# A chunked linear-attention and squared-ReLU kernel: half of W1 in two wider loads, u and w by other engines, and another order of all steps

## The chip, the core and the metric

The kernel runs on one core of a Trainium2 chip. The metric is device time in microseconds (us), as a median over runs; lower is better. Before the change it is 173.49 us (three runs, 173.22 to 173.87).

In the profile PE is TensorE's matmul unit, PEld its weight load, DVE is VectorE, ACT is ScalarE, POOL is GpSimd and SP is SyncE, which here only issues transfers. A "q" behind an engine's name (SPq, POOLq) is its sequencer, which waits and issues.

## What is computed

For 4 batches and 8 heads of 768 time steps with 48 channels, a recurrence with a decayed state, and then a two-layer network with a squared ReLU on its output (3072 rows of 384):

```python
for t in range(S):
    cur = einsum('bhd,bhe->bhde', u * k[t], v[t])
    y[t] = einsum('bhd,bhde->bhe', r[t], state + cur)
    state = w[:, :, None] * state + einsum('bhd,bhe->bhde', k[t], v[t])
x = y as (3072, 384)
h = maximum(x @ w_in, 0)          # w_in: 384 x 2048, called W1 in the kernel
out = h * h @ w_out               # w_out: 2048 x 384, called W2
```

Inputs and output are float32; the matmuls of the kernel take bfloat16.

## The kernel before

**Units.** The 768 steps are cut into 6 chunks of 128, which with 4 batches gives 24 units; unit i is batch i mod 4, chunk i div 4. Each unit goes through the same steps, each named by a method of class `Do`, with its unit behind it (`A.7` is step A of unit 7):

- `ld.r`, `ld.k`, `ld.v` (line 387) load the unit's 128 x 8 x 48 values, 192 KB in runs of 48 floats.
- `kh`, `rh` (424, 430) scale k and r by powers of w into `rk`. Units 0 to 3 read these powers from PSUM, where `WkQ` and `WtQ` write them; later ones from SBUF (`WkS`, `WtS`).
- `T` and `Tc` (454, 466) transpose r and k on TensorE and copy them to SBUF as `rkT`; from unit 7 on `XB` (473) does this by a transposing transfer.
- `A` (476) makes the products of k and r within the chunk, `Bm` (501) masks them, in two halves `.0` and `.1`; `Y` (509) multiplies with v (`vb`, line 451, is v as bfloat16) and adds the part from the state.
- `P0`, `P1`, `du`, `dv` (436 to 446) make the term with u: r times k, times u, summed over channels, times v. `xs` (559) adds it to Y.
- `U` (536) makes the unit's share of the state; `S0`, `ts`, `S` (566 to 572) carry the state on with the decay `WLm`.
- `X` and `xTc` (575, 580), or `xX` (584) by a transposing transfer, give x transposed.

**The network** works on groups of units: `GROUPS` makes group 0 and 1 of one unit each (units 0, 1) and groups 2 to 12 of two (units 2 and 3, 4 and 5, and so on). `F1.g.s` (587) is 12 matmuls of 128 columns for a group of one unit or 6 of 256 for one of two, `re` (599) takes the maximum with 0 and `sq` (606) squares. A group of one unit has 4 F1 steps, one of two has 8. F1.g.s of a group of two needs slice s of W1; of a group of one it needs slices 2s and 2s+1. `F2.i.f.4` (615) adds 4 of unit i's 16 products with W2, from slice f/4 of it; `os` (652) copies the sum and `out` (657) stores it. The last unit is done in two parts (`F2c`).

**The weights.** W1 is 8 slices of 256 columns. `lW.0.s` (393) loads a slice through SP, 384 KB in runs of 1 KB, into a staging buffer `st`, and `cW.0.s` (403) casts it; slice 2 is cast by the transfer itself, which GpSimd issues (`W.0.2`, line 416). W2's four slices come that way, too (`W.1.0` to `W.1.3`). `lQ.q` (400) can load slices 2q and 2q+1 at once; with `WIDE` empty it isn't used.

**w and u.** `w` (314) and `u` (323) load the two tables as rows, and the shuffles `shw`, `shu` (320, 329) spread them over all partitions. `wc` (361) loads w a second time, as a column, in two transfers of single elements, and `WLcol` (370) takes its power by 128.

**Fillers.** `Z.n.b` (643) does matmuls of the identity worth n times 128 columns into bank b, in 512-column matmuls and a rest of 128-column ones. Their result is not read.

**Order.** `ORDER` (line 24) is one list of 951 steps. Each is `name:engine/buffers`: A is ScalarE, D VectorE, G GpSimd, P TensorE, S SyncE's transfer queue; the digits choose buffers or PSUM banks. The loop at line 676 issues them in this order, so each engine runs its own steps in the list's order; semaphores enforce what the data and the buffers ask.

```python
for step in ORDER.split():
    what, how = step.split(":")
    ...
    getattr(Do, name)(E[eng[0]], *at, *map(int, eng[1:]))
```

The first steps of each engine that matter here, in the list before:

```
SP      ld.r.3 ld.k.0 ld.r.0 u ld.r.1 ld.k.3 ld.r.2 ld.k.1 ld.k.2 lW.0.1 ld.v.0 ld.v.3 lW.0.5 ld.v.1 lW.0.0 lW.0.4 ld.v.2 lW.0.6 lW.0.7 lW.0.3 wc ld.r.4 ld.k.4 ld.k.5 ld.r.5 ld.v.5
GpSimd  P0.0 P1.0 P1.3 vb.3 dv.3 dv.0 vb.1 P0.2 P1.2 dv.1 cW.0.4 W.0.2 dv.2 W.1.0 cW.0.3 WLm W.1.1 kh.4 W.1.2
VectorE shw shu rh.0 rh.3 kh.3 kh.0 du.0 P0.3 kh.1 rh.1 kh.2 du.3 P0.1 P1.1 rh.2 du.1 cW.0.1 Bm.0.1 Bm.1.0 Bm.0.0 Bm.3.1 Bm.3.0 xs.0 Bm.1.1 xs.3 xTc.0 du.2 xs.1 Bm.2.0 xTc.1 Bm.2.1 cW.0.6 cW.0.7 xs.2 xTc.2
TensorE Z.66.7 T.3 T.0 Z.22.7 A.0 T.1 A.1 A.3 U.3 T.2 Y.0 U.0 A.2 Y.3 X.0 Y.1 X.3 F1.0.0 X.1 F1.0.2 F1.1.2 F1.1.0 Y.2 U.2 F1.1.3 X.2 F1.0.3 F1.2.0 F1.2.3 F1.2.1 F1.0.1 F1.2.7 F1.2.6 F2.3.0.4
```

## Time and profile before

| what | value |
|---|---|
| median of three runs | 173.49 us (173.22 to 173.87) |
| the profiled execution | 174.07 us |
| its span, first to last instruction | 172.3 us |
| TensorE matmuls | 161.7 us busy, 94% of the span, x1691 |
| VectorE | 139.9 us, 81% |
| ScalarE | 104.5 us, 61% |
| GpSimd | 88.2 us, 51% |
| moved by transfers | 29.13 MB, mean 169 GB/s |

Matmuls overlap in TensorE's pipeline, so its busy time is no measure of a peak. Of an idle time only that of the engine that bounds a stage costs anything, so the profile is read by stages: busy time in stretches of the span, the chain of waits that ended last, and the waits of the engine that is full. The line numbers in the profile are those of the listing above.

### The profile page before, as it was taken

The numbers are of one execution on the slowest core, as the hardware profiler recorded it, in microseconds if no ns is written. First come the engines' busy times: TensorE is split into PE (matmuls) and PEld (weight loads), VectorE is DVE, ScalarE is ACT, GpSimd is POOL, SyncE is SP. The second block draws the span as 40 slices with busy tenths as digits, with TensorE's granted clock in tenths as the row PEclk, the third lists the DMA queues.
The fourth block names the chain that finished last, engine by engine and source line by source line (L and its number), as shares of the span: only waits on it lengthen the run. The fifth ranks groups of instructions, "written<-read, shape, count | busy, mean of one in ns | idle before, by whom it ended". The sixth has DMA issues, their size and how long they took to land.

```text
span 172.3 us, 4337 instructions
## 1 busy us (share of the span) xinstructions
PE 161.7 (94%) x1691; PEld 121.6 (71%) x1691; DVE 139.9 (81%) x272; ACT 104.5 (61%) x187; POOL 88.2 (51%) x105
## 2 busy tenths in 40 slices
PE   3976899999999997999999999999999999999993
PEld 1445788776787776777687696886686786878772
DVE  5599887569999996788999899779989889682731
ACT  3475477694599485467569276595596454553740
POOL 5425967215857497998339402879922872000000
PEclk9995699999999999999999999999999999999999
DMA  5999999999697998999999997999595963130322
GB/s 99 218 230 257 330 211 192 202 147 224 112 204 153 209 205 190 231 194 183 238 176 211 185 206 140 230 159 234 132 130 107 127 136 98 44 93 0 141 91 91
DMA packets 105588, 29.13 MB, mean 169 GB/s; under 512 B 98008, under 2 KB 105568, under 8 KB 105568
## 3 DMA queue, kind: packets, MB, share of 16 engines
q1 hardware_dynamic: 103672, 26.95, 76.2%
q0 software_dynamic: 1744, 1.77, 6.8%
q8 instruction: 13, 0.21, 0.5%
q10 hardware_dynamic: 152, 0.14, 0.2%
q14 instruction: 7, 0.06, 0.1%
HBM read 20.46 MB, written 4.72 MB: 146 GB/s over the span
## 4 chain that ended last, share of the span: by engine, by line
PE 71%; SPq 10%; DMA 7%; ACT 5%; DVE 2%; issue 2%; POOL 1%; POOLq 0%; ACTq 0%
PE bank L622 31%; PE bank L594 29%; SPq L388 5%; SPq L396 4%; DMA st<-in_moe_w_in_dram 4%; DMA ldv<-in_v_dram 3%; PE bank L494 3%; ACT hr L602 2%; PE bank L531 2%; ACT hq L609 2%; PE bank L527 2%; PE bank L552 2%; PE bank L636 2%; PE bank L578 1%; DVE S0W L567 1%
## 5 line engine op out<-in xcount | busy, mean ns | idle before, releaser
L594 PE MATMUL bank<-xT,W 128*128 128x256 bf16 (+1 forms) x624 | 71.2, 266 | 0.4 <-DVE W L288 0.3
L622 PE MATMUL bank<-W,hq 128*128 128x384 bf16 x368 | 68.5, 326 | 0.3 <-DVE S0W L567 0.3
L594 PEld LDWEIGHTS <-W 128*128 128x128 bf16 x624 | 56.1, 99 | 9.0 <-DVE W L288 0.5
L602 ACT ACTIVATE hr<-bank 128x512 bf16<-128x512 f32 x70 | 40.6, 593 | 27.5 <-PE bank L594 26.8
L609 ACT ACTIVATE hq<-hr 128x512 bf16<-128x512 bf16 x72 | 43.6, 626 | 7.3 <-DVE hr L604 6.1
L622 PEld LDWEIGHTS <-hq 128*128 128x128 bf16 x368 | 33.9, 98 | 19.2 <-ACT hr L602 0.5
L507 DVE TENSOR_TENSOR Bm<-bank,maskJT 128x512 bf16<-128x512 f32 x48 | 31.1, 678 | 0.6 <-PE bank L494 0.6
L604 DVE TENSOR_SCALAR hr<-bank 128x512 bf16<-128x512 f32 x26 | 17.6, 686 | 11.7 <-PE bank L594 9.7
L441 POOL TENSOR_TENSOR P<-P,ub 128x384 f32<-128x384 f32 x14 | 15.0, 1072 | 16.2 <-DVE P L437 15.9
L434 POOL TENSOR_TENSOR rk<-ldr,Wt 128x384 bf16<-128x384 f32 x13 | 13.8, 1063 | 7.8 <-DMA ldr<-in_r_dram 7.8
L449 POOL TENSOR_TENSOR dv<-ldv,du 128x384 f32<-128x384 f32 x16 | 13.9, 878 | 2.8 <-DVE du L444 2.8
L560 DVE TENSOR_TENSOR xs<-bank,dv 128x384 bf16<-128x384 f32 x24 | 13.1, 552 | 2.0 <-PE bank L531 0.9
L444 DVE TENSOR_REDUCE du<-P 128x8 f32<-128x384 f32 x24 | 12.9, 545 | 1.6 <-POOL P L441 1.3
L286 ACT COPY os<-bank 128x384 f32<-128x384 f32 x13 | 5.9, 487 | 13.4 <-PE bank L622 13.4
L573 POOL TENSOR_TENSOR S0W<-ts,WLm 128x384 bf16<-128x384 f32 x9 | 9.4, 1053 | 8.7 <-DVE ts L570 8.6
L428 POOL TENSOR_TENSOR rk<-ldk,Wkhat 128x384 bf16<-128x384 f32 x12 | 12.8, 1076 | 2.0 <-DMA ldk<-in_k_dram 1.9
L531 PE MATMUL bank<-vb,Bm 128*128 128x48 bf16 x192 | 11.6, 187 | 1.5 <-DVE Bm L507 0.9
L613 DVE TENSOR_TENSOR hq<-hr 128x512 bf16<-128x512 bf16 x24 | 12.4, 523 | 0.3
L288 POOL CAST vb<-ldv 128x384 bf16<-128x384 f32 x10 | 6.1, 606 | 12.7 <-DMA ldv<-in_v_dram 11.5
L437 POOL TENSOR_TENSOR P<-ldr,ldk 128x384 f32<-128x384 f32 x10 | 10.6, 1066 | 3.4 <-DMA ldr<-in_r_dram 3.4
L531 PEld LDWEIGHTS <-Bm 128*128 128x128 bf16 x192 | 9.9, 99 | 2.6 <-DVE Bm L507 1.7
L288 DVE COPY os<-bank 128x384 f32<-128x384 f32 (+2 forms) x12 | 6.2, 518 | 6.0 <-PE bank L622 2.7
(67 smaller groups left out, 163.7 us busy)
## 6 DMA issues: line engine op xcount, KB each, us to landing
ldr<-in_r_dram SPq DMA_DIRECT2D x24, 192.0 KB, 4.0
ldk<-in_k_dram SPq DMA_DIRECT2D x24, 192.0 KB, 3.7
ldv<-in_v_dram SPq DMA_DIRECT2D x24, 192.0 KB, 4.2
out_dram<-os SPq DMA_DIRECT2D x23, 192.0 KB, 2.3
st<-in_moe_w_in_dram SPq DMA_DIRECT2D x7, 384.0 KB, 5.6
W<-in_moe_w_out_dram POOLq DMA_DIRECT2D x4, 384.0 KB, 7.2
rkT<-rk SPq DMA_TRANSPOSE x17, 3.7
W<-in_moe_w_in_dram POOLq DMA_DIRECT2D x1, 192.0 KB, 5.1
```

The costliest lines, as they stand in the source:

```text
L434: e.tensor_mul(scaled("r", i), loaded("r", i), early("WtQ") if i < EARLY else Wt2)
L441: e.tensor_mul(t, t, ub)
L444: e.tensor_reduce(dub[slot[f"dv{i}"]], P0b[slot[f"P{i}"]], axis=mybir.AxisListType.X, op=ALU.add)
L449: e.tensor_mul(dvb[slot[f"dv{i}"]], loaded("v", i), t)
L507: e.tensor_mul(o, a, mask_b)
L531: e.matmul(y[:, hc, D * h : D * (h + 1)], m[h][:, hc, :], vb[:, 2 * hc + h, :], start=(i < B), stop=True, skip_group_check=True,)
L560: e.tensor_add(xsb[slot[f"xs{i}"]].rearrange("p (a b) -> p a b", a=HP), heads(bank(f"bY{i}"), 2 * D), dvb[slot[f"dv{i}"]].rearrange("p (a ...
L594: e.matmul(hp[:, fi, :], W1[f // 2][:, c, 128 * (f % 2) : 128 * (f % 2 + 1)], xt[:, c, :], start=(c == 0), stop=(c == CCH - 1), skip_group ...
L602: e.activation(hr, hp, AF.Relu)
L604: e.tensor_scalar_max(hr, hp, 0.0)
L609: e.activation(hq, hr, AF.Square)
L622: e.matmul(bank(f"bO{i}")[:, 0:d_model], hqb[slot[f"hq{g},{f // m}"]][:, at : at + L], W2[f // 4][:, f % 4, :], start=(summed[i] == 1), st ...
```

## The change

The same steps compute the same values. What differs:

- `WIDE = (2, 3)`: slices 4 to 7 of W1 come by `lQ.2` and `lQ.3`, two loads of 768 KB in runs of 2 KB, into two buffers `sw`, instead of four `lW`. The four casts read from there.
- `u` is issued by GpSimd instead of SP.
- `WCP = True`: `wc` is eight products on TensorE of a row of `logw` with a single 1, into a PSUM bank; `WLcol` then needs only one step for each half. The two transfers of single elements are gone.
- `st` has 5 buffers instead of 6, `hq` 29 instead of 30.
- `ORDER` is another list of 956 steps: other places, other engines and other buffers for nearly all. By engine: `re` 62 on ScalarE and 34 on VectorE (70 and 26 before); `P0` 14 on GpSimd and 10 on VectorE (10 and 14); `P1` 16 and 8 (14 and 10); `dv` 19 and 5 (16 and 8); `cW` 3 ScalarE, 1 VectorE, 3 GpSimd (2, 3, 2); `os` 16 ScalarE and 9 VectorE (13 and 12). Nine fillers worth 131 x 128 columns replace two worth 88.
- Other edits rewrite options that neither version uses (paired units, `DUO`, loads of two units at once), and the mask tile's name.

The first steps of each engine in the new list:

```
SP      ld.r.0 ld.k.0 ld.k.3 ld.r.3 ld.r.1 ld.k.1 ld.r.2 ld.v.3 ld.k.2 ld.v.1 ld.v.0 lQ.2 lQ.3 lW.0.0 ld.v.2 ld.r.5 ld.k.5 lW.0.1 ld.k.4 ld.r.4 lW.0.3 ld.v.4 ld.v.5 ld.v.7 ld.k.7 ld.r.7
GpSimd  P0.0 u P0.3 P1.3 P0.2 P1.2 vb.1 dv.0 cW.0.5 vb.0 dv.3 dv.1 WLm cW.0.0 dv.2 W.0.2 cW.0.1 P0.5 W.1.0 kh.4 rh.4 P0.4 W.1.1 W.1.2
VectorE shw kh.3 kh.0 rh.0 rh.3 rh.1 kh.1 P0.1 rh.2 shu P1.0 Bm.0.0 Bm.3.1 P1.1 du.0 Bm.0.1 du.1 Bm.1.1 kh.2 du.3 du.2 Bm.1.0 Bm.3.0 xs.0 xTc.0 xs.1 xs.3 Bm.2.0 Bm.2.1 S0.0 kh.5 rh.5 xs.2 xTc.2
ScalarE w tab logw WkQ WtQ WtS Tc.3 WkS Tc.0 WLcol vb.3 Tc.1 cW.0.4 Tc.2 cW.0.6 cW.0.7 re.0.3
TensorE Z.20.6 wc Z.15.6 T.0 T.3 Z.14.6 T.1 A.3 A.0 Z.4.4 A.1 Z.55.5 T.2 Z.5.1 Y.0 Z.12.1 A.2 Y.3 Z.2.6 X.0 Y.1 U.0 Z.4.7 F1.0.3 X.1 F1.0.2 U.1 X.3 F1.1.2 Y.2 F1.1.3 T.5 X.2 U.2 F1.0.0 F1.2.0 F1.2.1 F1.1.0 F1.2.7 F1.2.6 T.4 F1.2.5 F1.2.4 A.4 A.5 F1.2.3 F1.0.1 F1.1.1 F2.0.0.4
```

```diff
-WIDE = ()
-WCP = False
-POOLS = dict(ldr=7, ldk=7, ldv=7, st=6, rk=7, P0=5, dv=5, vb=8, rkT=7, Bm=6, xs=5, hr=6, hq=30, os=4, ts=2, xT1=2, xT2=3)
+WIDE = (2, 3)
+WCP = True
+POOLS = dict(ldr=7, ldk=7, ldv=7, st=5, rk=7, P0=5, dv=5, vb=8, rkT=7, Bm=6, xs=5, hr=6, hq=29, os=4, ts=2, sw=2, xT1=2, xT2=3)
 ORDER = """
-w:A ld.r.3:S/0 ld.k.0:S/0 ld.r.0:S/1 shw:D u:S P0.0:G/0 shu:D tab:A logw:A WkQ:A/0 WtQ:A/1 rh.0:D/0 ld.r.1:S/2 ld.k.3:S/1
...
+ld.r.0:S/0 w:A tab:A ld.k.0:S/0 ld.k.3:S/1 ld.r.3:S/1 ld.r.1:S/2 shw:D ld.k.1:S/2 logw:A ld.r.2:S/3 P0.0:G/0 WkQ:A/1 Z.20.6:P
+wc:P/0 ld.v.3:S/0 WtQ:A/2 u:G kh.3:D/0 ld.k.2:S/3 WtS:A kh.0:D/1 P0.3:G/2 ld.v.1:S/1 rh.0:D/1 rh.3:D/0 Z.15.6:P T.0:P/3
+ld.v.0:S/2 rh.1:D/2 T.3:P/4 Tc.3:A/0 kh.1:D/2 lQ.2:S/0 P0.1:D/1 Z.14.6:P T.1:P/5 WkS:A rh.2:D/3 lQ.3:S/1 A.3:P/6/7 Tc.0:A/1
+shu:D lW.0.0:S/0 P1.0:D P1.3:G WLcol:A A.0:P/4/2 vb.3:A/1 ld.v.2:S/3 Bm.0.0:D/0 Tc.1:A/2 P0.2:G/3 Bm.3.1:D/1 ld.r.5:S/4
...
```

The options that this change switches on were there before:

```python
def wc(e):
    for h in range(H if WCP else 0):
        e.matmul(
            bank("wc")[64 * (h % 2) : 64 * (h % 2) + D, h // 2 : h // 2 + 1], logw[0:1, h, :], one,
            start=True, stop=True, skip_group_check=True,
        )
    for h in range(0 if WCP else 2):
        e.dma_start(out=wcol[64 * h : 64 * h + D, :], in_=w.rearrange("(a e) d -> e d a", e=2)[h])
def lQ(e, q):
    e.dma_start(out=swb[slot[f"wq{q}"]], in_=w_in_t[:, :, 512 * q : 512 * (q + 1)])
```

More of the change, by code (lines that the diff above doesn't have):

```diff
@@ L525, in Y @@
             for hc in range(HP):
[L526 removed]
+                if not fresh[i]:
                     e.matmul(
[L528 removed]
+                        y[:, hc, :], t[:, hc, :], S0W[UNITS[i][0]][:, hc, :], start=True, stop=False, skip_group_check=True,
                     )
@@ L659, in out, with blocks @@
             t = osb[slot[f"os{i}"]]
+            b, p = UNITS[i]
             if i < PAIRED:
                 o = bass.AP(
-                    tensor=out.tensor, offset=out.offset + ((i - i % 2 + half) * S + i % 2) * d_model,
-                    ap=[[2 * d_model, L // 2], [1, d_model]],
+                    tensor=out.tensor, offset=out.offset + (b * S + i % 2) * d_model, ap=[[2 * d_model, L], [1, d_model]],
                 )
-                e.dma_start(out=o, in_=t[rows[half], :])
+                e.dma_start(out=o, in_=t)
             else:
-                e.dma_start(out=out_v[(i % B) * NCH + i // B][:, c], in_=t[:, c])
+                e.dma_start(out=out_v[b * NCH + p][:, c], in_=t[:, c])
+    def blocks(e, o, s, t):
+        ks, rt = rkTb[slot[f"rkT{s}"]], rkTb[slot[f"rkT{t}"]]
+        for hc in range(HP):
+            for h in range(2):
+                q = slice(64 * h, 64 * h + D)
+                e.matmul(
+                    heads(bank(f"{o}{h}"), 128)[:, hc, :], ks[q, HP + hc, :], rt[q, hc, :],
+                    start=True, stop=True, skip_group_check=True,
+                )
     def part(half):
@@ L681 @@
         held = HELD.get(name, [])
[L682 to L685 removed]
+        if name in ("xTc", "xX"):
             held = [h.format(group_of[at[0]][0]) for h in held]
[L687 to L688 removed]
         else:
```

396 lines of the change are left out of this document (163 added, 233 removed).

## The prediction

> **What bounds the kernel now.** I read the page first, for the clock and the transfers, then busy time by stretch, then TensorE's waits after the start, then the chain that ended last.
>
> ```profile
> span 172.3 us, 4337 instructions
> ...
> PEclk9995699999999999999999999999999999999999
> DMA  5999999999697998999999997999595963130322
> ```
> ```profile
> 5.00:10.00 5.00, 5.00 (x35) 2.63 (x33) 3.79 (x9) 2.17 (x4) 2.43 (x3) 1.00 1.10 225
> 10.00:15.00 5.00, 2.75 (x42) 1.92 (x41) 4.96 (x11) 2.73 (x4) 1.59 (x3) 0.84 0.91 234
> 15.00:20.00 5.00, 4.29 (x58) 3.59 (x56) 4.55 (x10) 3.51 (x5) 3.84 (x6) 0.50 1.06 293
> ...
> 20.00:22.00 2.00, 1.50 (x23) 1.28 (x22) 1.77 (x5) 0.67 (x2) 2.00 (x3) 0.94 1.07 332
> ...
> 60.00:80.00 20.00, 19.07 (x197) 14.63 (x195) 16.70 (x31) 12.83 (x24) 18.02 (x20) 1.00 1.04 202
> ...
> 120.00:140.00 20.00, 19.98 (x203) 15.23 (x202) 17.69 (x35) 13.32 (x24) 12.19 (x14) 1.00 0.83 141
> ```
> The columns of the second fence are the stretch, its length, then busy time of TensorE's matmuls, its weight loads, VectorE, ScalarE and GpSimd, the granted clock, the DMA share and GB/s. Two stages show. In the first some 25 us VectorE (4.96 of 5 us busy) and the transfers (share about 1.1) are full while TensorE waits, with half its clock from 15 to 20 us. Later TensorE is full: 19.98 of 20 us.
>
> ```profile
> PE bank L531 <- DVE Bm L507: 0.9, 1, 0.9
> PE bank L622 <- DVE S0W L567: 0.3, 1, 0.3
> ```
> These are all of TensorE's waits between 26 and 168 us, by who ended them: 1.2 us. So a new order wins little more than that there; the rest must come from the start.
>
> ```profile
> 31.71 0.67 PE bank L594 x12
> 32.38 0.65 PE bank L622 x4
> ...
> 34.99 0.45 PE bank L464 x8
> ...
> 39.96 0.55 PE bank L494 x16
> ...
> 60.87 5.29 DMA ldv<-in_v_dram
> 66.18 0.51 ACT vb L286
> ...
> 67.94 0.20 PE bank L531
> ```
> The chain (start, length, what) prices TensorE's steps: an F1 step 0.66, an F2 step of four matmuls 0.65 (either is a piece, 0.66 below), T 0.45, A 0.28 (two took 0.55). It shows the longer wait, too: a load of v takes 5.29 us, then come its cast, a mask product and Y.
>
> **The change, part by part.** The rows of the start, by start and length, and the groups that price its steps:
>
> ```profile
> 2.71 5.53 PE L648 MATMUL bank<-identity 128*128 128x512 bf16 x16 [2.71 <-POOL identity masks.py:199]
> 2.77 0.82 SPq L324 DMA_DIRECT2D urow<-in_u_dram  x1
> ...
> 4.27 0.52 ACT L333 ACTIVATE logw<-wb 128x384 f32<-128x384 f32 x1 [0.63 <-DVE wb L321]
> ...
> 5.79 0.01 DVE L330 LOAD_MASK_SELECT ub<-urow  x1 [1.55 <-DMA urow<-in_u_dram]
> ...
> 5.94 1.00 POOL L437 TENSOR_TENSOR P<-ldr,ldk 128x384 f32<-128x384 f32 x1 [2.78 <-DMA ldr<-in_r_dram]
> ...
> 7.55 1.02 DVE L428 TENSOR_TENSOR rk<-ldk,bank 128x384 bf16<-128x384 f32 x2 [0.28 <-DMA ldk<-in_k_dram]
> ...
> 9.08 1.24 PE L648 MATMUL bank<-identity 128*128 128x512 bf16 x5
> 9.28 1.01 ACT L286 COPY rkT<-bank 128x1024 bf16<-128x1024 bf16 x1 [2.83 <-PE bank L464]
> ...
> 13.48 0.94 DVE L288 CAST W<-st 128x768 bf16<-128x768 f32 x1
> ...
> 18.86 1.82 SPq L368 DMA_DIRECT2D wcol<-in_w_dram  x2
> ...
> 19.34 1.27 PE L594 MATMUL bank<-xT,W 128*128 128x128 bf16 x12
> ...
> 22.95 0.76 POOL L422 DMA_DIRECT2D W<-in_moe_w_out_dram  x1
> ...
> 25.40 0.36 DVE L288 COPY xT<-bank 128x384 bf16<-128x384 bf16 x1 [0.43 <-PE bank L578]
> ...
> 30.25 1.46 PE L622 MATMUL bank<-W,hq 128*128 128x384 bf16 x8 [0.28 <-DVE S0W L567]
> ```
> ```profile
> L507 DVE TENSOR_TENSOR Bm<-bank,maskJT 128x512 bf16<-128x512 f32 x48 | 31.1, 678 | 0.6 <-PE bank L494 0.6
> ...
> L441 POOL TENSOR_TENSOR P<-P,ub 128x384 f32<-128x384 f32 x14 | 15.0, 1072 | 16.2 <-DVE P L437 15.9
> ...
> L560 DVE TENSOR_TENSOR xs<-bank,dv 128x384 bf16<-128x384 f32 x24 | 13.1, 552 | 2.0 <-PE bank L531 0.9
> L444 DVE TENSOR_REDUCE du<-P 128x8 f32<-128x384 f32 x24 | 12.9, 545 | 1.6 <-POOL P L441 1.3
> ...
> W<-in_moe_w_out_dram POOLq DMA_DIRECT2D x4, 384.0 KB, 7.2
> ...
> W<-in_moe_w_in_dram POOLq DMA_DIRECT2D x1, 192.0 KB, 5.1
> ```
> Landing of the loads. The third load (ld.r.0) landed by 5.94, the fifth by 7.55; a load of 196.6 kB at 225 GB/s is 0.87 us, so load n lands at 5.94 + 0.87(n-3). A W1 slice of 393 kB at 332 GB/s takes 1.2 us. Four loads of slices 4 to 7 become two of twice the size; nothing here shows 2 KB runs, so between the price per byte of the small loads (225 GB/s, 3.5 us each) and less than the slices' 2.4 us I take 2.4, the nearest row. In the new queue of SP (11 loads, lQ.2, lQ.3, lW.0.0, ld.v.2, r.5, k.5, lW.0.1, k.4, r.4, lW.0.3) that gives v.0 at 12.9, lQ.2 15.3, lQ.3 17.7, lW.0.0 18.9, v.2 19.8, k.5 21.5, lW.0.1 22.7, r.4 24.5, lW.0.3 25.7. The two issues that SP loses (0.82 for u, 1.82 for the column of w) were issue time beside a DMA share of 1.07: nothing, hidden by the transfers; were the queue empty there, 2.6.
>
> u by GpSimd's queue: issued behind P0.0, which needs the second load (5.1), so at 6.1. By SP it landed within 5.79 - 2.77 = 3.0; the loads of GpSimd's queue took 5.1 and 7.2. So it lands at 9.1 to 13.3; the size is that of the 3.0, so 9.1. VectorE's turn at it comes at 10.2 (below): cost 0, at worst 3.1, for all of VectorE's list is queued behind the wait.
>
> Column of w by TensorE: eight small products that no row shows. Between the 0.03 of an A matmul (0.55/16) and the 0.35 of a 512-wide one at the start (5.53/16) they take 0.3 to 2.8 us from logw's end (4.27 + 0.52 = 4.8). T.0 can't come before rh.0 at 7.4 and Z.15 is between (4 wide ones, 1.2): cost 0 to 1.4, taken 0, by the small matmul. What it frees on SP is in the part above.
>
> VectorE decides the start. From kh.3 to xTc.2 its new list has 13 products like kh, rh, P0 and P1 at 0.51 (two took 1.02), du x4 at 0.55, Bm x8 at 0.68, xs x4 at 0.55, two xTc at 0.36, S0 0.51 and the shuffle 0.58: 6.6 + 2.2 + 5.4 + 2.2 + 0.7 + 0.5 + 0.6 = 18.2. (Two casts of 0.94 have left it.) It starts with the third load, 5.9, and has two waits: k.1, 0.2, and A.0, whose Tc.0 stands behind Tc.3 and WkS on ScalarE (T.3 ends 8.6; 1.0 + 0.6 + 1.0 + 0.3 makes 11.5 against VectorE's 11.3), 0.2. With some 0.02 between its 33 instructions that makes 5.9 + 18.2 + 0.4 + 0.7: xTc.2 ends at 25.2; before, it ended at 25.40 + 0.36 = 25.8. So group 2, on which most F1 steps hang, comes 0.6 earlier.
>
> The fillers, 131 units of 128 columns instead of 88, come ahead of all F1 steps. Z.55.5 is the one that could hurt: 13 wide matmuls at 0.25 (1.24/5) or 0.35, so 3.3 or 4.6 us from A.1's end at 13.3. T.2 behind it needs kh.2, the 18th step of VectorE's list, done at about 16.9. It costs 0 to 1.0 on Tc.2 and, behind that on ScalarE, the casts of slices 6 and 7 (0.9 each), so F1.0.3 starts at 20.2 to 21.5. Five pieces (3.3) are to be done before group 2 at 25.2: done at 24.8 at the latest, so nothing.
>
> [...]
>
> From there on both orders list pieces. New: 2.0, 2.1, 1.0, 2.7, 2.6, T.4, 2.5, 2.4, A.4, A.5, 2.3, 0.1, 1.1, which is 10 x 0.66 + 0.45 + 0.55 = 7.6, so the first F2 stands at 32.8 with 15 pieces, T.4, T.5, A.4 and A.5 done. Before, F2 began at 30.25 behind 12 pieces and did (32.8 - 30.25)/0.66 = 3.9 more: 15.9 pieces. The new order has 15 + (0.9 + 0.55)/0.66 = 17.2, so it is 1.3 pieces ahead: **-0.9**. Slice 0 of W2 must be there: lW.0.1 22.7, cast 0.9, P0.5 1.0, issue at 24.6, 7.2 to land: 31.8, under 32.8. (Before: 22.95 + 7.2 = 30.15, and F2 at 30.25: that landing set F2's start.)
>
> The full stage. TensorE computes the same, so only its waits can change. The order gives loads more room: between the load of v and its Y, the smallest number of pieces over units 4 to 23 rises from 0 to 9 (median 12 to 20.5; for the waiting unit 8 from 6 to 16), between a DMA transpose and its A from 0 to 7. That takes away the 0.9 us wait. VectorE loses 3.3 us in all (8 more re, fewer P0, P1, dv, cW, os), GpSimd gets 6 more, ScalarE 2; the cover for these is TensorE's full stage, and without it each would cost its own length. A load's own time is not in the order, so some of that room will be used up: between the whole 0.9 and nothing I take two thirds, **-0.6**. One buffer fewer for st and for hq: st now takes three loads for five buffers, and hq comes round after 29 squares, as many F1 steps, 19 us; both 0 under TensorE's own work. The tail is the same steps: 0.
>
> Sum: span 172.3 - 0.9 - 0.6 = 170.8. The profiled execution took 174.07, of which 1.77 lie around the span; the median of the runs shown is 173.49, so by the runs 173.49 - 1.5 = **172.0**.
>
> **The rivals.** (A) The start gains more: VectorE's list without the waits and gaps I added, 18.2 from 5.9, ends at 24.1, and all behind it comes 1.1 earlier: 170.9. For it: VectorE was kept full already, 4.96 of 5 us. Against: slices 1 and 3 land at 22.7 and 25.7 whatever VectorE does.
>
> (B) No gain: the start gives its 0.9 back, since four loads of units 4 and 5 (3.5 us) now stand ahead of lW.0.3, and the full stage keeps waits of 1.2 in all: 173.5. For it: GpSimd already had 18.02 of 20 us in the row for 60 to 80 us and gets more.
>
> (C) Slower: GpSimd's queue becomes the bound of the start. W.1.0, kh.4 and rh.4 stand behind cW.0.1, which waits for lW.0.1, which stands behind two more loads than its place suggests. At my times rh.4 ends at 24.6 + 0.8 + 2 x 1.07 = 27.5 and T.4 is due at 25.2 + 5 x 0.66 = 28.5; so it decides from 1.0 us late, when T.4 stops TensorE with F1.2.5 and all F2 behind it, and makes the kernel slower than before from 1.0 + 1.5 = 2.5 late. If W.0.2, on the same engines, holds lW.0.1 back by its whole 5.1 us, the end is 4.1 later: 176.1. Against: the two loads put ahead of lW.0.1 are 0.87 each, and beside W.0.2's transfer the page still shows a share of 9 tenths and more to divide, so W.0.2 would have to take all of it.
>
> (D) u lands as late as the W2 loads, 7.2: VectorE stands 3.1 us, 175.1; with 5.1 it stands 1.0, 173.0. For it: those are the only rows of that queue; against: they move 192 KB and more.
>
> **How the numbers follow.** Forecast 0.38, A 0.18, B 0.20, C 0.16, D 0.08. A measurement of this kernel tells about 0.5% (0.87 us) from no change, so faster is below 172.6 and slower above 174.4. Of the forecast's 0.38, whose own range is 171.2 to 173.0, 0.32 is below 172.6; with A 0.50 faster. B, the rest of the forecast and the milder half of D make 0.28 the same. C and half of D, with a little of B, make 0.22 slower. The range leaves a tenth at each end: 169.9, somewhat below A, to 175.3, between C's point of decision and its whole price.
>
> **What would show it.** Right: xTc.2 near 25 us, the first F2 matmul at 32 to 34 us with 15 F1 steps before it, no wait of TensorE over 0.5 us after 34. The shuffle of u without a wait, the eight small products within 2 us, slice loads of lQ at 2.4 us each. Wrong: VectorE idle at the shuffle (D), T.4 waiting for GpSimd's rk (C), new waits on Bm or xT after 40 us (B), xTc.2 at 24 (A).

## The result, and the profile after

| | before | after |
|---|---|---|
| median of 5 runs | 173.22 us (172.15 to 173.87) | 177.93 us (176.98 to 178.08) |
| ratio after to before | | 1.0251, interval 1.0217 to 1.0284 |
| profiled execution, and its span | 174.07 us, 172.3 us | 178.01 us, 176.3 us |

The change makes the kernel 2.5% slower. The prediction was 172.0 us and faster, with a range up to 175.3. Every ratio here leaves out runs that took over 1.5% more than the fastest of the same kernel; where that leaves few, the ratio of the medians of all runs stands beside it.

The profile of the changed kernel answers to the rows shown of before. First its page:

```profile
span 176.3 us, 4400 instructions
...
PEclk9999999999999999999999999999999999999998
DMA  5999999999289988999999998998947623013212
```

Then busy time by stretch (columns as in the prediction), and one stretch of the kernel before beside it:

```profile
10.00:15.00 5.00, 2.96 (x33) 1.37 (x28) 4.75 (x10) 2.88 (x6) 3.90 (x4) 1.00 0.97 232
15.00:20.00 5.00, 3.93 (x50) 2.29 (x48) 4.02 (x8) 2.26 (x3) 3.86 (x7) 1.00 1.08 329
...
30.00:36.00 6.00, 2.97 (x42) 2.31 (x40) 5.63 (x9) 3.07 (x6) 3.71 (x5) 1.00 1.19 202
36.00:60.00 24.00, 24.00 (x256) 17.90 (x254) 19.21 (x36) 16.54 (x31) 10.77 (x12) 1.00 0.88 171
...
120.00:140.00 20.00, 19.45 (x182) 14.27 (x180) 17.00 (x32) 8.56 (x16) 9.66 (x10) 1.00 0.76 147
```
```profile
30.00:36.00 6.00, 5.75 (x55) 4.54 (x56) 4.05 (x10) 4.51 (x8) 1.70 (x2) 1.00 1.09 183
```

The half clock of the old start is gone: 1.00 where it was 0.84 and 0.50. Yet from 30 to 36 us TensorE is busy for 2.97 us, where it was for 5.75. The timeline of the changed kernel there, columns start, length, engine, line, what, and in brackets the idle time before it and what ended that:

```profile
26.23 3.80 PE L536 MATMUL bank<-xT,W 128*128 128x128 bf16 x42 [0.57 <-POOL W L287]
27.10 0.76 POOL L408 DMA_DIRECT2D W<-in_moe_w_out_dram  x1
27.18 4.03 DVE L427 TENSOR_TENSOR P<-P,ub 128x384 f32<-128x384 f32 x1 [0.56 <-POOL P L423]
27.88 1.01 POOL L414 TENSOR_TENSOR rk<-ldk,Wkhat 128x384 bf16<-128x384 f32 x1
28.84 0.99 POOL L420 TENSOR_TENSOR rk<-ldr,Wt 128x384 bf16<-128x384 f32 x1
29.80 0.99 POOL L423 TENSOR_TENSOR P<-ldr,ldk 128x384 f32<-128x384 f32 x1
...
31.13 0.68 DVE L546 TENSOR_SCALAR hr<-bank 128x512 bf16<-128x512 f32 x1
...
31.86 1.47 PE L536 MATMUL bank<-xT,W 128*128 128x256 bf16 x12 [1.39 <-DVE hr L546]
32.90 0.63 ACT L551 ACTIVATE hq<-hr 128x512 bf16<-128x512 bf16 x1 [3.56 <-DVE hr L546]
...
33.91 1.00 ACT L285 COPY rkT<-bank 128x1024 bf16<-128x1024 bf16 x1
34.97 0.62 PE L616 MATMUL bank<-rkT 48*128 48x128 bf16 x16 [1.64 <-ACT rkT L285]
...
37.53 1.46 PE L564 MATMUL bank<-W,hq 128*128 128x384 bf16 x8
```

One product of VectorE, chunk 5's P1 at line 427, takes 4.03 us. The seven other products of this kind on VectorE take 0.54 to 0.87 us in this profile. Beside it GpSimd runs three products of chunk 4 in a row (kh, rh, P0). VectorE is free 0.4 us after the last of them ends (30.79). Behind the product stand the `re` steps that empty TensorE's banks, so TensorE waits 1.39 us for one. ScalarE waits 3.56 us for another, and the copy rkT that A needs is queued behind that on ScalarE: TensorE waits 1.64 us more. The first F2 comes at 37.53 us, 7.3 us later than before, of which the prediction had 2.6 as the new order's plan (32.8).

To compare the two over the whole span, I added up TensorE's matmuls up to a time t, without the fillers, each at the length that it has back to back (an F2 matmul of 384 columns 162.5 ns, four in 0.65 us in the chain of before; an F1 matmul of 256 columns 109.3 ns, thirty in 3.28 us there). t minus that sum is called the idle time so far below: waits, fillers and half clock together. Both kernels hold 149.0 us of such work.

```
t, us         25    30    36    60    70   100   130   160
before      17.0  17.2  17.4  17.8  18.9  19.6  20.1  20.3
after       17.2  17.9  21.2  21.4  21.4  21.9  23.2  24.0
```

By 36 us the changed kernel is 3.8 us behind, and at 160 us 3.7. In between it wins back 1.5 by 100 us (the old order's wait of 1.1 at 68 us among it) and loses 1.4 from there on. TensorE's waits of the changed kernel, by who ended them (total, times, longest), show both:

```profile
PE bank L616 <- ACT rkT L285: 1.8, 2, 1.6
PE bank L536 <- DVE hr L546: 1.4, 1, 1.4
PE bank L536 <- DMA xT<-xs: 1.1, 3, 0.6
```

The last row is F1 (L536) waiting for chunks of x that a transfer transposes, three times, at 101, 125 and 149 us by the trace.

### The profile page after: what moved, and what is told of

It is laid out like the page before. It is cut to its first block, busy times and chain, and to the rows that moved or that the text cites. A ratio compares the mean times of both kernels' runs of the same rounds, so it can differ in the third digit from the quotient of the medians.

```text
span 176.3 us, 4400 instructions
## 1 busy us (share of the span) xinstructions
PE 162.6 (92%) x1723; PEld 122.4 (69%) x1723; DVE 144.2 (82%) x265; ACT 105.1 (60%) x191; POOL 94.0 (53%) x110
## 4 chain that ended last, share of the span: by engine, by line
PE 63%; DMA 12%; SPq 6%; DVE 6%; issue 6%; ACT 3%; POOL 2%; DVEq 0%; POOLq 0%
PE bank L564 27%; PE bank L536 27%; DMA xT<-xs 7%; SPq L362 5%; DMA st<-in_moe_w_in_dram 5%; PE bank L616 2%; DVE hr L546 2%; PE bank L484 2%; PE bank L480 2%; PE bank L578 2%; PE bank L494 1%; ACT hq L551 1%; DVE xs L502 1%; PE bank L520 1%; ACT hr L544 1%
## 5 line engine op out<-in xcount | busy, mean ns | idle before, releaser
L536 PE MATMUL bank<-xT,W 128*128 128x256 bf16 (+1 forms) x624 | 71.2, 264 | 3.1 <-DVE hr L546 1.4
L536 PEld LDWEIGHTS <-W 128*128 128x128 bf16 x624 | 55.9, 98 | 13.1 <-issue 3.0
L551 ACT ACTIVATE hq<-hr 128x512 bf16<-128x512 bf16 x73 | 44.2, 628 | 21.1 <-DVE hr L546 20.2
L544 ACT ACTIVATE hr<-bank 128x512 bf16<-128x512 f32 x62 | 36.2, 595 | 24.2 <-PE bank L536 23.3
L459 DVE TENSOR_TENSOR Bm<-bank,mask 128x512 bf16<-128x512 f32 x48 | 31.2, 681 | 3.0 <-PE bank L616 1.9
L546 DVE TENSOR_SCALAR hr<-bank 128x512 bf16<-128x512 f32 x34 | 22.9, 683 | 6.3 <-PE bank L536 6.2
L435 POOL TENSOR_TENSOR dv<-ldv,du 128x384 f32<-128x384 f32 x19 | 16.9, 895 | 15.7 <-DVE du L430 15.5
L427 POOL TENSOR_TENSOR P<-P,ub 128x384 f32<-128x384 f32 x16 | 18.0, 1126 | 12.7 <-DVE P L423 9.4
L423 POOL TENSOR_TENSOR P<-ldr,ldk 128x384 f32<-128x384 f32 x14 | 14.3, 1020 | 3.9 <-DMA ldr<-in_r_dram 2.0
L414 POOL TENSOR_TENSOR rk<-ldk,Wkhat 128x384 bf16<-128x384 f32 x10 | 10.7, 1066 | 5.7 <-DMA ldk<-in_k_dram 4.4
L590 PE MATMUL bank<-identity 128*128 128x512 bf16 x30 | 9.5, 445 | 3.6 <-POOL identity masks.py:199 2.7
L512 DVE TENSOR_TENSOR ts<-bank,S0W 128x384 f32<-128x384 f32 x16 | 8.8, 548 | 3.6 <-PE bank L494 3.6
L285 ACT COPY os<-bank 128x384 f32<-128x384 f32 (+1 forms) x16 | 7.4, 466 | 6.2 <-PE bank L564 4.9
```

The lines of the kernel that those rows point to most:

```text
L423: e.tensor_mul(P0b[slot[f"P{i}"]], loaded("r", i), loaded("k", i))
L427: e.tensor_mul(t, t, ub)
L435: e.tensor_mul(dvb[slot[f"dv{i}"]], loaded("v", i), t)
L459: e.tensor_mul(Bmb[slot[f"Bm{i}{h}"]], heads(bank(f"bA{i}{h}"), 128), masks(0))
L536: e.matmul(hp[:, fi, :], W1[f // 2][:, c, 128 * (f % 2) : 128 * (f % 2 + 1)], xt[:, c, :], start=(c == 0), stop=(c == CCH - 1), skip_group ...
L544: e.activation(hr, hp, AF.Relu)
```

## Experiments on the start

Theory L: VectorE's product with two operands in SBUF stands while GpSimd's products read SBUF. Such a longer time is called the lock below. Medians of before differ between chips (173.87 us on one, 175.33 on another), so each run below goes by its ratio to runs of before on the same chip.

**The lock alone.** A program with nothing but a GpSimd product that opens the gate, n GpSimd products, and one VectorE product behind the gate (the kernel's own work is left out).

```diff
+nc.gpsimd.tensor_mul(gate, last, y)
+for j in range(n):
+    nc.gpsimd.tensor_mul(side[j], x, y)
+nc.vector.tensor_mul(done, gate, y)
```

> The disputed cost by itself: the whole computation is left out. In each of ten segments GpSimd makes a gate tile of 128 x 384, and right behind it in its queue n more steps; VectorE makes one product that needs the gate. Names: r0, r1, r2, r4, r8 are 0 to 8 GpSimd products that read SBUF, w4 four GpSimd memsets, iss2 two transfers that GpSimd issues, one4 and ps4 four products beside a VectorE step with one operand in SBUF (a maximum) or one in SBUF and one in PSUM; r4b repeats r4. Theory L: VectorE's product takes about 0.55 + n x 1.0 us in r0 to r8 (0.55, 1.5, 2.5, 4.5, 8.5) and 0.55 or less in one4 and ps4. If only the GpSimd instruction that is running can hold it, r1 to r8 all take at most 1.5. If operands in SBUF don't matter, all take 0.55. For w4 and iss2 theory L leaves open whether writing or issuing holds it; the changed kernel's P1.5 began beside an issue (27.10) and did not get through, so iss2 is expected to hold it, up to 2 us.

Timeline of it: one product beside, eight, four with the operand from PSUM, four memsets.

```profile
4.37 0.99 POOL L58 TENSOR_TENSOR side<-x,y 128x384 f32<-128x384 f32 x1
4.45 1.33 DVE L64 TENSOR_TENSOR doner<-gater,y 128x384 f32<-128x384 f32 x1 [1.10 <-POOL gater L55]
...
15.04 7.95 POOL L58 TENSOR_TENSOR side<-x,y 128x384 f32<-128x384 f32 x8
15.12 1.33 DVE L64 TENSOR_TENSOR doner<-gater,y 128x384 f32<-128x384 f32 x1 [3.73 <-POOL gater L55]
...
28.85 0.55 DVE L68 TENSOR_TENSOR doneps<-gateps,pt 128x384 f32<-128x384 f32 x1 [3.73 <-POOL gateps L55]
...
33.60 0.56 DVE L64 TENSOR_TENSOR donew<-gatew,y 128x384 f32<-128x384 f32 x1 [4.20 <-POOL gatew L55]
```

VectorE's product begins 0.08 us after GpSimd's and takes 1.33 us, whether one or eight stand in the row. With one in the row it ends 0.42 us after that one (5.78 and 5.36). With one operand in PSUM, or memsets beside it, it took its own 0.55 to 0.56. Two expectations failed: beside two transfers that GpSimd issues it took 0.56, not up to 2 us, and a maximum with its one operand in SBUF took 1.13 beside four products, not 0.55 or less (its length alone was not measured). So the lock is there, but in these trials a product that came second stood for one GpSimd product only (1.33 us beside one, two, four and eight). That doesn't make 4.03 us.

**Chunk 5's product late (p1late), slice 1 of W1 earlier (slice1first), and both.** The product with u and its sum go behind a later `re` on VectorE; the load of slice 1 goes ahead of chunk 5's r and k.

```diff
-... P1.5:D F1.2.1:P/3 ... du.5:D/4 ... re.2.5:D/2 A.4 ...
+... F1.2.1:P/3 ... re.2.5:D/2 P1.5:D du.5:D/4 A.4 ...
```
```diff
-... ld.r.5:S/4 ... ld.k.5:S/4 ... lW.0.1:S/1 ...
+... lW.0.1:S/1 ld.r.5:S/4 ... ld.k.5:S/4 ...
```

> The changed kernel with P1.5 and du.5 ten steps later on VectorE, behind re.2.5, so that P1.5 comes when GpSimd issues the W2 loads and no longer runs kh.4, rh.4 and P0.4 back to back. Theory L (a VectorE product with both operands in SBUF stands while GpSimd runs instructions without a gap; P1.5's 4.03 us held up re.0.0, re.1.0 and with them TensorE): P1.5 takes under 1.7 us, TensorE's two waits of 1.4 and 1.6 us near 31 and 34 us shrink to under 1 us together, and the kernel is 2 to 3 us faster than the changed one, 175 to 176 us. Theory Q (GpSimd's own list comes late behind the cast of slice 1, and T.4 and F2 with it): nothing changes on GpSimd, so 177.9 within 0.5.

> The changed kernel with lW.0.1 ahead of ld.r.5 and ld.k.5 in SP's queue, nothing else. Slice 1 should land some 1.7 us earlier than 25.25 and GpSimd's list behind its cast come as much earlier. Theory Q: the kernel is 1.7 to 2.5 us faster, 175.4 to 176.2. Theory L: P1.5 still stands for about 4 us beside the same three GpSimd steps; only the wait of 0.57 us for the cast goes, so 177.0 to 177.6.

> Both edits. Theory L: the two gains add, 174.2 to 175.3 us, and useful TensorE work by 36 us is within 1 us of the kernel before, instead of 3.8 us behind. Theory Q: like slice1first alone, about 175.8.

p1late: 1.0229 (1.0145 to 1.0312). The long product is gone (no P1 of VectorE over 0.80 us), and the idle time so far at 36 us is 19.8 in place of 21.2; at 160 us it is 24.3, as bad as ever. slice1first: 178.35 and 179.19 us in the two runs that count, against 175.0 on average of before (1.021, too few for an interval; by the medians of all 1.032). Its product began beside a GpSimd product that already ran and took 1.35 us, not the 4 that theory L expected; the idle time is 19.6 at 36 us and 24.2 at 160. both: 1.0252 (1.0175 to 1.0329), 19.3 and 26.5. So the repairs give the start back 1.4 to 1.9 of the 3.8 us, less than theory L expected, and by 160 us the profiles have lost it again. By the times this is clear for both only: 1.9 us would make about 1.014, below its interval, but the 1.017 that 1.4 us would make lies inside that of p1late.

**The lock again, with VectorE first (lock2).** The product now begins ahead of the row of GpSimd products, behind a PSUM product that moves its start.

```diff
 nc.gpsimd.tensor_mul(gate, last, y)
+nc.gpsimd.dma_start(out=wt, in_=w_out_t[q % 3])   # or two memsets
 for j in range(n):
     nc.gpsimd.tensor_mul(side[j], x, y)
+nc.vector.tensor_mul(scrap[:, 0:w], gate[:, 0:w], pt[:, 0:w])
 nc.vector.tensor_mul(done, gate, y)
```

> Leaves the whole computation out. Ten trials of one VectorE product with two SBUF operands (0.56 us alone) that is begun first, ahead of a row of GpSimd products: GpSimd's gate product, then one transfer issue (or two memsets) of about 0.75 us, then n products; VectorE's product stands directly behind the gate (a), or behind a PSUM product of 192 (b, d, f, i: 6 behind), 288 (j) or 384 columns (c, e, g, h) that moves its start towards GpSimd's first product. Theory F (a product of VectorE that a row of GpSimd products catches while it runs stands until the whole row is done): about 0.56 in a and where it ends in time, and where GpSimd's first product begins within it about 3.3 to 4 us with three, 1.3 to 1.6 with one, 6 to 7 with six; the issue or the memsets ahead make no difference. Rival G (VectorE stands behind the one GpSimd product that runs, as in the first trial of this kind): at most 1.4 in all. Rival H (it is the issue ahead that holds it): 3 or more behind issues only, 0.6 to 1.4 behind memsets.

Timeline of trials a (ends in time), e (one product), f (three, behind memsets) and i (six, behind an issue):

```profile
2.78 0.56 DVE L65 TENSOR_TENSOR donea<-gatea,y 128x384 f32<-128x384 f32 x1 [0.65 <-POOL gatea L55]
3.64 2.89 POOL L62 TENSOR_TENSOR side<-x,y 128x384 f32<-128x384 f32 x3
...
20.37 0.55 DVE L65 TENSOR_TENSOR donee<-gatee,y 128x384 f32<-128x384 f32 x1
20.63 1.14 POOL L62 TENSOR_TENSOR side<-x,y 128x384 f32<-128x384 f32 x1
...
23.03 3.68 DVE L65 TENSOR_TENSOR donef<-gatef,y 128x384 f32<-128x384 f32 x1
23.41 2.88 POOL L62 TENSOR_TENSOR side<-x,y 128x384 f32<-128x384 f32 x3
...
35.90 6.42 DVE L65 TENSOR_TENSOR donei<-gatei,y 128x384 f32<-128x384 f32 x1
36.16 5.74 POOL L62 TENSOR_TENSOR side<-x,y 128x384 f32<-128x384 f32 x6
```

A product that the row caught while it ran stood in three trials until the whole row was done: 3.68 us with three (f, and j behind an issue), 6.42 with six (i). Each of the three ended 0.42 us after the row's last product (in f 26.71 and 26.29). It did not always. Trials e and h with one product, and g with three that began 0.17 us into it, kept 0.55 and the row gave way (in e 1.14 for 0.99); c let go after 2.64; b and d, where the row began 0.47 us in, took 0.72 and 0.55. In trials b to j the starts of product and row lie 0.17 to 0.48 us apart, and each was tried once. Theory F, as that expectation calls it, holds in this weaker form; that only the running product counts (G), or the issue ahead (H), falls. In trials f and i VectorE began first by the trace, by 0.38 and 0.26 us, and was held all the same (3.68 and 6.42 us), by products that began later.

**In place: without the reading (noread), and another begin (w1late).** Chunk 4's kh, rh and P0 become two memsets each (chunk 4 is computed from zeros); or the issue ahead of them goes behind them.

```diff
 def kh(e, i):
+    if i == 4:
+        for _ in range(2):
+            e.memset(scaled("k", i), 0.0)
+        return
...
```
```diff
-... S0.2:D W.1.0:G ... P1.5:D ... kh.4:G/5 ... rh.4:G/5 ... P0.4:G/0 ...
+... S0.2:D ... P1.5:D ... kh.4:G/5 ... rh.4:G/5 ... P0.4:G/0 W.1.0:G ...
```

> The changed kernel with chunk 4's three GpSimd products (k and r scaled, r times k) replaced by two memsets each, so that chunk 4 is computed from zeros. Theories F and G: chunk 5's product with u takes 0.55 us on VectorE in place of 3.5 to 4.0, TensorE's waits of 1.4 and 1.6 us at 31 to 35 us go, idle time so far at 36 us 18.5 to 19.0 in place of 20.2 to 21.2. If something other than the reading holds it: 3 us or more as before.

> The changed kernel with the issue of slice 0 of W2 moved behind chunk 4's three GpSimd products, so that these follow chunk 5's product r times k at once and chunk 5's product with u begins beside a GpSimd product that already runs. Theory G, and F for a start behind a product that runs: 1.3 to 1.4 us in place of 3.5 to 4.0; rival H (the issue is what holds it): 0.56 to 1.4; a row of products that holds it whenever it starts: 3 us. Time: with 1.4 the start gains 1.5 to 2 us, which the middle takes back by theory Q: ratio 1.020 to 1.026.

Timeline rows of noread, then of w1late:

```profile
27.79 0.56 DVE L439 TENSOR_TENSOR P<-P,ub 128x384 f32<-128x384 f32 x1 [1.21 <-POOL P L435]
```
```profile
26.87 0.99 POOL L414 TENSOR_TENSOR rk<-ldk,Wkhat 128x384 bf16<-128x384 f32 x1
27.15 1.13 DVE L427 TENSOR_TENSOR P<-P,ub 128x384 f32<-128x384 f32 x1
27.83 1.31 POOL L420 TENSOR_TENSOR rk<-ldr,Wt 128x384 bf16<-128x384 f32 x1
```

Without the reads the product took 0.56 us; begun beside a product that already ran, 1.13, and it ended 0.42 us after that one (28.28 and 27.86). noread alone proves little, for in one profile below (spfill) the product took 0.56 with the reads in place. What ties the long product to the row is where it ends: 0.42 us after the row in the changed kernel (31.21 and 30.79), and also in the profiles of two runs below with the same start, outact (30.13 and 29.71) and afterdelay (30.56 and 30.13). So it is shown that the row holds it. Not shown is why a product of 0.56 us was not done when the row began 0.70 us after it.

The idle time so far at 36 us is 19.6 in noread and 19.8 in w1late. So the long product is worth 1.4 to 1.6 of the start's 3.8 us (p1late and noread). The 19.6 is above the 18.5 to 19.0 expected of noread, since slices 1 and 3 of W1 landed late there too (two waits of TensorE for their copies, 1.2 and 1.0 us). Again the end gains nothing: w1late 1.0285 (1.0177 to 1.0393; by the medians of all runs 1.035), noread one run of 179.41 us beside 174.78 of before.

## Experiments on the middle

After the first F2 the trace shows SyncE's queue nearly without a break from 50 to 120 us (8.3 to 10.0 of each 10 us are issues of transfers), and one hole before that in the changed kernel:

```profile
38.89 4.07 SPq L362 DMA_DIRECT2D ldk<-in_k_dram  x2
47.83 1.34 SPq L450 DMA_TRANSPOSE rkT<-rk  x1
```

The queue stands from 42.96 to 47.83 us for XB.7, whose input VectorE makes late, with loads behind it that could go. Theory Q says that this queue sets the middle.

**Loads into the hole (spfill, bothfill, fillp1).** Four loads go ahead of XB.7: alone, with both repairs of the start, and with the late product alone.

```diff
-... P0.7:D/1 XB.7:S/6 ... out.2:S ld.r.9:S/1 ... ld.v.6:S/2 ... ld.k.12:S/3 ... ld.k.11:S/4 ...
+... P0.7:D/1 ld.r.9:S/1 ld.v.6:S/2 ld.k.12:S/3 ld.k.11:S/4 XB.7:S/6 ... out.2:S ...
```

> The changed kernel with four loads (r of chunk 9, v of 6, k of 12, k of 11) put ahead of chunk 7's transposing transfer in SyncE's queue. Theory Q (the middle is set by SyncE's in-order queue): between 50 and 120 us SyncE issues nearly back to back, and in the changed kernel and in the three repaired starts it has the same 33 or 34 issues out at 50 us and 43 or 44 at 60 us, however far TensorE is; it stood from 42.96 to 47.83 us behind that transfer. The four loads fill the hole, SyncE is 3 or 4 issues ahead at 50 us, and TensorE's 1.1 us of waits on the transposed x between 100 and 150 us go: ratio to before 1.010 to 1.018 in place of 1.025. Rival W (TensorE's own losses set the end, SyncE has slack): no change, 1.025.

> Both repairs of the start (chunk 5's product and sum late on VectorE, slice 1 of W1 ahead of chunk 5's r and k) and the four loads ahead of chunk 7's transposing transfer. Theory Q: the 1.9 us that the two repairs gained by 36 us (idle time so far 19.3 in place of 21.2) are no longer lost in the middle: ratio 1.000 to 1.012. Rival W: as the two repairs alone, 1.025.

> The four loads ahead of chunk 7's transposing transfer and chunk 5's product with u late on VectorE, W1's slice 1 where the change has it. The start's idle time at 36 us 18.5 to 19.8, and SyncE 3 issues ahead at 50 us. Theory Q with theory F (the start's stall and SyncE's hole each cost the whole, so both have to go): ratio 1.008 to 1.014, and less spread than the run with the loads alone, whose product stalled in some executions. Rival W: 1.014 to 1.022, as either alone.

Busy time from 40 to 50 us in the changed kernel, in before and in spfill (last three columns: clock, DMA share, GB/s):

```profile
40.00:50.00 10.00, 10.00 (x99) 6.97 (x98) 8.45 (x16) 4.72 (x9) 3.09 (x3) 1.00 0.63 115
```
```profile
40.00:50.00 10.00, 10.00 (x119) 7.75 (x117) 9.65 (x17) 5.65 (x12) 6.95 (x8) 1.00 0.94 171
```
```profile
40.00:50.00 10.00, 10.00 (x80) 7.01 (x79) 7.55 (x14) 4.47 (x10) 4.30 (x5) 1.00 1.14 193
```

The hole is filled: 193 GB/s in place of 115. spfill comes to 1.0149 (1.0089 to 1.0210), as Q expects, but its runs scatter (175.35 to 179.97), and by the medians of all six it is 1.020, above Q's range. In the profiled one the long product didn't occur: it began 27.06 and took 0.56 us, where the same code took 3.76 and 3.52 in the profiles of the next two runs. bothfill, 1.0216 (1.0165 to 1.0267), and fillp1, 1.0246 (1.0188 to 1.0304), contradict Q: they hold the repair of the start and of the hole, and end no better. So the hole is not what the repairs are lost to.

**Stores from ScalarE (outact).**

```diff
-... out.2:S ... out.3:S ... out.0:S ... out.4:S ...
+... out.2:A ... out.3:A ... out.0:A ... out.4:A ...
...
```

> The changed kernel with eleven of the output stores (chunks 0 and 2 to 11) issued by ScalarE in place of SyncE. SyncE is rid of eleven issues of 0.57 us and of its waits for their copies (11.3 and 8.4 us in all). Theory Q: SyncE gets ahead by 6 us over the middle, the waits on the transposed x go: ratio 1.010 to 1.020. Rival D (the bytes on the DMA engines set the middle, not the issuing): 1.025. Rival W: 1.025, or more if ScalarE is held up by the copies that the stores wait for.

1.0201 (1.0129 to 1.0273) from three runs, and 1.025 by the medians of all six: at the edge of Q's range, with the rivals' 1.025 inside its interval. By the trace SyncE issued for 57.4 us between 50 and 120 where it had issued for 63.5, and 23.76 MB had moved by 120 us, as in the changed kernel (23.78). Fewer issues on the queue didn't move more bytes. SyncE's waits for copies stayed, against the expectation (11.2 and 7.4 us): they belong to the later stores. TensorE's waits for transposed x fell from 1.1 to 0.3 us, but those for rkT, which ScalarE copies, rose from 1.8 to 2.7.

**A delay put in (afterdelay, beforedelay).** Fillers of TensorE: 2.15 us in the new order, where they ran from 38.2 us on, and 3.44 us in the old, where the same piece comes earlier and they ran from 32.8 us on.

```diff
-... sq.2.3:D2/9 F1.2.2:P/4 ...
+... sq.2.3:D2/9 Z.40.4:P F1.2.2:P/4 ...
```
```diff
-... F2.1.0.4:P/1 F1.2.2:P/2 ...
+... F2.1.0.4:P/1 Z.64.2:P F1.2.2:P/2 ...
```

> The changed kernel with 2.15 us of filler matmuls (ten of 512 columns) put into TensorE's list ahead of the eighth-last piece of the first layer of group 2, at about 38 us. Theory Q: TensorE has slack behind SyncE in the middle, less than half shows at the end: ratio 1.025 to 1.031. Rival W: all of it shows, 1.037.

> The kernel before with 3.44 us of filler matmuls (sixteen of 512 columns) put into TensorE's list ahead of the same piece as in the other delay, at about 38 us: TensorE's useful work is then as late as in the changed kernel at 40 us (idle time so far 20.9 against 21.2). Theory M (the middle of the old order has as little room as the new one's, so the start alone makes the difference): all of it shows, 1.018 to 1.022. Theory D (in both, transfers that nothing holds up run on meanwhile, so that a late start is partly made up): 1.008 to 1.014; then the rest of the 4.4 us is the new order's middle.

afterdelay: 1.0319 (1.0276 to 1.0363) in place of 1.0251 (on another chip); of 1.24% put in 0.7% shows, and the whole, 1.0375, lies outside the interval. With the interval of the 1.0251 counted too, 0.1 to 1.2% shows, so the share is hardly known; the result lies between the ranges of Q and W. beforedelay: 1.0259 (1.0209 to 1.0309); of 1.96% put in all shows, and more. That a delay shows where TensorE is full is no surprise; what comes on top are waits on transposed x, 1.9 us in three between 95 and 160 us, where the kernel before has none. So the old order does not make a late start up, and with TensorE as late at 40 us (20.7 against 21.2) it is as slow as the changed kernel (1.0251). A start that is 3.4 us late is enough for the whole loss.

**Fewer bytes (noout, beforenoout).** Eleven output stores of 197 KB are left out, in the new order together with the late product, and in the old.

```diff
-... out.2:S ... out.3:S ... out.0:S ... out.4:S ...
+...
```

> Chunk 5's product with u late on VectorE (as in the first repair, 1.023 there), and eleven of the output stores (chunks 0 and 2 to 11) left out: 2.2 MB fewer of the 24 MB that are moved by 120 us. Theory D (the transfers' bytes set the middle: by 120 us 23.0 to 24.1 MB had been moved in the changed kernel's variants, and the fewer, the longer the time): the waits on transposed chunks between 95 and 150 us, 2 to 4 us in these variants, go: 1.000 to 1.012. Rival W (the middle's waits come from the order of the work, not from bytes): 1.018 to 1.025.

> The kernel before without the same eleven output stores (chunks 0 and 2 to 11). Theory D for both orders: the old order's middle, which loses 2.9 us from 40 to 160 us, 1.1 of it at 68 us for a late load of v, loses less: 0.985 to 0.994. If bytes set only the new order's middle: 0.995 to 1.003.

noout: 1.0054 (1.0018 to 1.0089), where the late product alone gave 1.0229; its only wait of TensorE over 0.15 us between 95 and 160 us was one of 0.25. beforenoout: 0.9920 (0.9885 to 0.9956). Both lie in the ranges of theory D, that the bytes set the middle. The gain looks larger in the new order, but with the intervals it is 0.9 to 2.7% there against 0.4 to 1.2%. Leaving a store out also takes its issue out of SyncE's queue. outact took the issues out and left the bytes, and gained 0.5% or nothing, though ScalarE paid for them there; so the bytes are the likelier cause, but they were not changed alone.

**One transfer's place (xxfirst).** In fillp1, whose longest wait was this row of TensorE's waits:

```profile
PE bank L536 <- DMA xT<-xs: 2.0, 2, 1.6
```

the transposing transfer of chunk 16 goes ahead of a store and a load that stood between it and that of chunk 17.

```diff
-... xX.17:S/1 ... xs.16:D/3 ... out.8:S ... ld.v.21:S/0 ... xX.16:S/1 ...
+... xX.17:S/1 ... xs.16:D/3 xX.16:S/1 ... out.8:S ... ld.v.21:S/0 ...
```

> The four loads ahead of chunk 7's transposing transfer, chunk 5's product late on VectorE (1.025 there), and the transposing transfer of chunk 16 right behind that of chunk 17, ahead of the store of chunk 8 and the load of v of 21, behind which it stood. If TensorE's wait at 125 us (1.8 us in that run) comes from the place in SyncE's queue: the wait falls to 0.5 or less and the ratio to 1.014 to 1.020. If the transfers themselves are late: no change, 1.02 to 1.025.

1.0161 (1.0113 to 1.0209), and no wait at 125 us. That wait came from the place in the queue. By these ratios this run and spfill are the best of the new order's variants that compute everything; none beats the kernel before.

The middle in one table: idle time so far at 40 and 160 us, what lies between, and the megabytes moved by 120 us (GB/s of twelve stretches of 10 us, added up).

```
              40 us  160 us  lost   MB by 120 us   span
before         17.5   20.3    2.8      23.90       172.3
after          21.2   24.0    2.8      23.78       176.3
spfill         19.0   21.5    2.5      24.10       173.9
xxfirst        20.3   23.3    3.0      23.44       175.7
bothfill       20.0   23.3    3.3      23.77       175.7
w1late         20.0   24.0    4.0      23.59       176.3
p1late         20.2   24.3    4.1      23.51       176.6
outact         20.2   24.3    4.1      23.76       176.7
afterdelay     22.5   24.7    2.2      23.48       177.0
slice1first    19.7   24.2    4.5      23.64       176.6
fillp1         19.7   24.3    4.6      23.73       176.7
noread         19.8   25.3    5.5      23.38       177.7
both           19.8   26.5    6.7      23.04       178.8
parts2         17.5   22.8    5.3      23.59       175.2
beforedelay    20.7   25.8    5.1      22.91       177.8
```

Each row is one profile, and runs of one kernel differ by 1 us and more (the changed kernel's five by 1.1, spfill's six by 4.6), so small differences between rows say nothing. In the new order the longest spans mostly go with the fewest bytes. Bytes by 120 us can also be few because TensorE is late and its buffers come free late (beforedelay has 22.91 where before has 23.90); the two runs without stores are the better evidence that bytes count.

## Experiments on the named parts

**The parts in the old order (parts, parts2).** `st` has three buffers here, one for each load that still uses it.

```diff
-... u:S ... lW.0.5:S/1 cW.0.5:A ... lW.0.4:S/3 cW.0.4:G ... lW.0.6:S/4 lW.0.7:S/5 ... wc:S ...
+... u:G ... wc:P/1 T.3:P/2 ... lQ.2:S/0 cW.0.5:A ... cW.0.4:G ... lQ.3:S/1 ...
```
```diff
-... wc:P/1 T.3:P/2 ... lQ.2:S/0 cW.0.5:A ... cW.0.4:G ...
+... wc:P/4 T.3:P/2 ... lQ.2:S/0 cW.0.4:G cW.0.5:A ...
```

> The kernel before with the change's named parts alone put into its own order: slices 4 to 7 of W1 in two loads of two slices each, u on GpSimd's queue, the column of w made by sixteen matmuls on TensorE (three transfers fewer on SyncE). Theory O (the new order costs the 4.4 us, the parts nothing): 0.995 to 1.005. Rival P (a part itself costs: the double load holds up what stands behind it in the queue, or the copies that read it are slower): 1.01 or more.

> The parts alone in the old order again, placed so that they delay nothing there: the column of w in a bank that is free (in the first try it shared one with a table, and the first transposes came 1.2 us later), the first double load at the place of slice 4 in place of slice 5, and slice 5's copy on ScalarE behind slice 4's (in the first try ScalarE stood 2.26 us for it ahead of a copy of v, and the clock stayed at 0.50 until 24.9 us). Theory O (the parts cost nothing where they are placed well; the order costs the 4.4 us): 0.995 to 1.006. Rival P (the parts cost by themselves): 1.010 or more again.

parts: 1.0139 (1.0099 to 1.0179). There the column of w shared its bank with the table WtQ and wrote over four of its columns, so r of the first chunks was scaled by other values; the steps are the same. Half clock lasted to 24.9 us, and 1.5 us were lost in the start:

```profile
20.00:25.00 5.00, 4.99 (x58) 4.86 (x56) 4.39 (x10) 1.70 (x4) 4.98 (x7) 0.51 1.17 262
```

parts2 mends that: its idle time so far is that of before up to 60 us (17.8), and at 70 us it is 1.2 us ahead, since the old wait at 68 us is gone. It still comes to 1.0134 (1.0088 to 1.0180): all is lost from 85 us on. Rival P is right by its number, but not by its mechanism: no part holds up the start. The old order's own transposing transfer xX.12 shows how. Busy time from 90 to 100 us and the time from issue to landing (smallest, median, largest of one transfer), parts2 and then before:

```profile
90.00:100.00 10.00, 8.56 (x89) 5.78 (x88) 8.82 (x17) 4.94 (x10) 5.37 (x6) 1.00 0.92 170
...
DMA to landing us min/median/max: 5.0/5.0/5.0
```
```profile
90.00:100.00 10.00, 10.00 (x118) 7.46 (x115) 9.43 (x20) 6.48 (x14) 6.55 (x7) 1.00 1.01 205
...
DMA to landing us min/median/max: 2.9/2.9/2.9
```

It is issued at 94.8 and 94.9 us, behind the same transfers, and lands at 99.8 in place of 97.9; F1 waits 1.1 us. Why the engines moved 170 GB/s there and not 205 stays open.

## Why the prediction was wrong, step by step

- **What bounds the kernel.** "Later TensorE is full" held for the profile that was read. That it would stay so under another order did not: the delay in the old order alone brought up 1.9 us of waits on transposed x, so the transfers landed with little to spare.
- **Landing of the loads.** The price of a double load was right: lQ.3 landed 2.56 us after lQ.2 (2.4 predicted). The places were too early: lQ.2 16.9 (15.3), lQ.3 19.5 (17.7), slice 1 25.3 (22.7), slice 3 29.1 (25.7). The rate of 332 GB/s taken for the slices held from 15 to 20 us (329), not after (211 from 20 to 25). It cost TensorE 0.57 us, in the row of 26.23.
- **u and the column of w: right.** u landed at 8.9 (9.1), VectorE came to it at 10.3 without a wait, and the column's products (sixteen matmuls in the trace) took 0.80 us at 4.95. The prediction's rival D (u late) didn't occur.
- **VectorE's list: nearly right.** xTc.2 ended at 25.6 (25.2; before 25.8).
- **The fillers: right.** F1.0.3 came at 20.7 (20.2 to 21.5). The clock was 1.00 from 10 to 20 us, where before it was 0.84 and 0.50; the prediction's sum has no term for that. What it gave ahead of 26.23 us was hidden by the wait there for slice 1's copy (0.57 us).
- **The pieces behind 25.2 us: the step that failed.** They were priced at TensorE's 7.6 us, with VectorE and GpSimd at the lengths of single rows, so that the start was to give 0.9 us; by 36 us it had cost 3.8. The first F2 came at 37.5 and not at 32.8. The product P1.5 took 4.03 us in place of 0.51, because the new order puts a row of three GpSimd products beside it, and behind it TensorE waited 1.39 and 1.64 us. The lock trials and the ends of product and row show that cause. It is not the whole: with the product short, 2.2 to 2.4 of the 3.8 us remain (noread, p1late), some of it the late slices 1 and 3. That a start as late is worth the 4.4 us is shown by beforedelay in the old order. In the new order no run got more than 2.2 us of it back. The prediction's rival C looked at the right row, GpSimd's kh.4 and rh.4, but for its lateness: rh.4 ended at 29.8 and T.4 followed without holding TensorE. The harm came from the row's reading beside VectorE's product (4.03 us with it, 0.56 in noread).
- **The full stage, -0.6: failed.** The changed kernel was 3.8 us behind at 36 us and 3.7 at 160, so the term came to next to nothing. The wait of 1.1 us at 68 us went, as said. But the order's larger margins were counted in TensorE's pieces, and new waits on transposed x, 1.1 us, took it back. The runs without stores (1.0054 where 1.0229 was, and 0.9920) make it likely that this stage goes by the bytes that are moved, which has no term in the prediction. The named parts, put at nothing, cost 1.3% in the old order, all of it from 85 us on (parts2). Why transfers land late there, and why a repaired start gains little or nothing at the end, stays open. The prediction's rival B named such waits, without a price above 1.2.
